# Layer 1's blocks 2 to 5 as two more pairs, and the second batch's transform beside the first pairs

## The chip, the cores and the metric

The kernel runs on one core of a Trainium2 chip. The metric is the device time in microseconds of one execution. Times are medians of several runs; the profile is of one execution, taken by the hardware profiler.

## The reference

The inputs are x (2 batches of 3008 tokens, 256 channels), a filter in the frequency domain, and two layers of weights, each 256 to 2048 to 256. What is computed:

```
X = rfft(x, axis=1);  y = irfft(X * (filt_r + 1j * filt_i), n=3008, axis=1)
h = y @ w_in1;  g = where(h >= 1, h, where(h <= -1, 0, (h + 1)**2 / 4));  z = g @ w_out1
h = z @ w_in2;  out = (h * sigmoid(h)) @ w_out2
```

All is in fp32. Both batches together are 6016 tokens.

## The kernel before, in words

**Precision.** TensorE has a slow fp32 form and a fast one that rounds (fp32r). Most products use the fast one: each operand is split into a rounded part and its remainder, and three matmuls are summed (`triple`): high by high, high by low, low by high. Splitting takes one ScalarE copy (rounding) and one subtraction on VectorE or GpSimd.

**The transform.** The 3008 tokens of a batch are 47 x 64. An item is 16 channels of one batch, 32 items in all. It goes through three products: `fwd_n1`, a VectorE transpose (`turn_fwd`), `fwd_n2`, the filter (`filter_`, two products on VectorE with the filter and with its signed half, `signs` on GpSimd), a swap of halves on ScalarE with an addition on GpSimd (`swap_add`), `inv_n2`, and a transpose into the store Z (`turn_inv`). The last product of the inverse, `last_stage`, is made for each block of tokens just before the block is used. `HEAD` items (17) run at the start, in fp32, one after another. The other 15 run in the split form beside layer 1; their stages stand in `BSTAGES`, as offsets from a start that moves on by `SP` / 10 slots an item. There they use the rotating ring of four PSUM banks `h` and, for the padded inverse, the bank `b1` (`clear_pads`).

**Layer 1.** The tokens are 12 blocks of about 500, two to a pair (`PAIRS`). The hidden 2048 columns are 16 weight blocks (`NFC`). Blocks 0 to 5 (`NS` = 6) run directly, in 96 slots: a slot is one block of tokens and one weight block, with six matmuls up (`up`), the activation (ramp and square on ScalarE, minimum and maximum on VectorE), a split, and six matmuls down (`down`) five slots later. Each block is made ready by `prep_x`.

**Pairs.** Blocks 6 to 11 run as pairs. A step (`step`, `Group`) takes one pair of blocks and two weight blocks, and computes the four up products by seven (Strassen's scheme in Winograd's form), 21 matmuls in place of 24; its down part stays direct in layer 1, 24 matmuls, those of the step before, put between the products (`gap`). The operands of a pair are sums of blocks (`sum_x`), split into a ring of stores (`split_x2`, `rest_x2`); the sums of weights are made beforehand (`sum_first`, `round_first`, `rest_first`). A step has three kinds of PSUM banks of the ring `h`: b, d and c. Bank b holds the running sum: the first product (`start`) goes into b, ScalarE copies it into d, product A12 is added in d; in b follow S2, a copy out (`snap`), S1, a second copy out, and S4. Bank c takes S3 and A22. Bank b alternates between two banks from step to step, so that the next step can start while the last product is still read. The fourth bank is thus the other b, which is also lent to `last_stage`.

**Layer 2** runs all six pairs, with seven products up and seven down, 42 matmuls a step, 48 steps. Its weights come as 64-bit numbers: they are fetched, turned into fp32 (`read_weight`, `form_weight`), put into DRAM (`put_weight`), and later fetched in pairs, summed, split and stored again (`stage2`, `sums2`, `round2`, `rest2`, `store2`).

**Order.** TensorE's instructions run in the order of the program. For the other engines a planner (`Planner`) holds the order: every instruction has a cost and a due time worked out back from its users, and the planner gives each engine, until a mark, the instruction that can start earliest, or one with an earlier due time that can start soon after. The agenda (`at`, `due`) sets the slot, or the quarter of a step, at which a piece of work enters the program. `NB` is the first slot's number, `GA` that of the first step of pairs (four numbers a step), `END` that of the transform's end.

Of the kernel before, what the change touches and what calls it, by code (L numbers as in the profile page):

```python
# [9 lines left out]
F32 = mybir.dt.float32  # L10
# [25 lines left out]
PAIRS = (502, 502, 500, 502, 502, 500)  # L36
# [55 lines left out]

class Op:
    __slots__ = ("engine", "fn", "need", "users", "busy", "until", "port", "due", "done", "at", "left")

    def __init__(self, engine, fn, busy, until, port):
        self.engine, self.fn, self.busy, self.until, self.port = engine, fn, busy, until, port
        self.need, self.users, self.due, self.done, self.at = [], [], 0.0, None, None


class Planner:
# [3 lines left out]
    def __init__(self, nc):  # L105
# [4 lines left out]
        self.pipe = 0.0  # L110
        self.given = 0
# [22 lines left out]
    def places(cls, ap):  # L134
# [5 lines left out]
        if end - at > 2048:  # L140
            cols, u = [(at % 512) // 32], (0, 16)
        else:
# [24 lines left out]
    def put(self, engine, method, call, args, kwargs):  # L167
# [22 lines left out]
        op.left = sum(o.done is None for o in op.need)  # L190
        op.at = len(self.ops)
# [99 lines left out]
def tile_fft_conv_moe_moe(  # L291
# [13 lines left out]
    HEAD, LAG, EARLY = 17, 5, 12  # L305
    PRODUCT = (0, 15, 16)
    SP, NBX, SZ = 27, 8, 7
# [32 lines left out]
    make_ring("xb", 2, mp, [128, 2, PMAX], F32R)  # L340
# [18 lines left out]
    x2d = dram.tile([2, 128, NTOK], F32, name="x2d")  # L359

    w2d = [dram.tile([128, 512], F32, name=f"w2d{f}") for f in range(NFC)]
# [12 lines left out]
    def fetch_weight(m, f):  # L374
        w_in, w_out = ((w_in1, w_out1), (w_in2, w_out2))[m]
        raw = rot("early" if m == 1 and f < EARLY else "raw")
# [35 lines left out]
    def split_weight(m, f, pool):  # L412
# [5 lines left out]
        (nc.vector if f in (1,) else nc.gpsimd).tensor_tensor(wl, a, wh.bitcast(F32), ALU.subtract)  # L418
# [5 lines left out]
    def clear_pads(tag):  # L424
        zps.clear()
        for j in range(2 if tag == "a" else 1):
# [55 lines left out]
    def fwd_n1(i):  # L482
        st[i] = rot("h")
# [11 lines left out]
    def fwd_n2(i):  # L495
        ps = rot("h")[:, :XS]
# [15 lines left out]
    def swap_add(i):  # L512
# [7 lines left out]
        nc.gpsimd.tensor_tensor(yf, yf, s, ALU.add)  # L520
        st[i] = y

    def inv_n2(i):
        z = zps[i % len(zps)][:, :, :K1]
# [7 lines left out]
    def turn_inv(i):  # L532
# [3 lines left out]
            zps[i % len(zps)].rearrange("p d (u w) -> p d u w", w=2),  # L536
# [3 lines left out]
    NS = 6  # L540
# [46 lines left out]
    def crowded(t):  # L587

        n = 0
        for j in range(t, t + NEAR):  # L590
            n += sum(fn in (fwd_n1, fwd_n2) for fn, _ in agenda.get(j, ()))
            n += sum(fn is load_block for fn, _ in agenda.get(j, ())) * 2
            c, f = slots[j - NB] if j < GA else (0, 0)
            n += 2 * (f == (15 if c == 0 else 8) and c not in (1, NS - 1))
        return n > ROOM + (1 if B1 <= t < END else 0)

# [26 lines left out]
    def evict(o, to, ring="ob"):  # L623
# [787 lines left out]
```

## Time and profile before

| | |
|---|---|
| runs | 1078.92, 1078.98, 1079.11 us; median 1078.98 |
| profiled execution | span 1077.9 us from the first to the last instruction; its whole time isn't given apart |
| granted TensorE clock | 1.000 |
| TensorE matmuls | 4795, busy 1071.2 us |
| VectorE / ScalarE / GpSimd | busy 917.6 / 895.5 / 230.2 us |
| DMA | 131.95 MB, mean 122 GB/s |

Busy times are unions of an engine's instructions. Matmuls are pipelined and their ends are modelled, so that TensorE can look busy where it does not go at its full pace; how far one start lies behind the other tells more. All instructions of the kernel are issued through one helper and have one line, L172; they are told apart by the names of their tiles: h, o_a and o_b are PSUM banks, gh and gl the two parts of an activation, wh, wl, sh and sl those of weights and their sums, xr and xb those of operands, hl those of the transform, and names such as g, u, c, we, rawb and sl_g are free slots that hold products of a step. PE is TensorE, ACT ScalarE, DVE VectorE, POOL GpSimd, SP the engine that issues most transfers.

### The profile page before, as it was taken

How to read it: one execution, taken by the hardware profiler on the slowest of the kernel's cores; microseconds unless marked ns; L12 is line 12 of the kernel's file. 1: busy time of each engine (PE TensorE's matmuls, PEld its weight loads, DVE VectorE, ACT ScalarE, POOL GpSimd, SP SyncE). 2: the span in 40 equal slices, each digit the busy share in tenths (PEclk: the TensorE clock that was granted, in tenths of full speed). 3: DMA queues.
4: the chain of work that ended last, by engine and by line, in shares of the span. 5: the costliest groups of instructions: out<-in, count | busy, mean ns of one | idle time of the engine just before them, and what ended most of it. 6: DMA issues, size and time to landing. Idle time of an engine off the chain costs nothing.

```text
span 1077.9 us, 14639 instructions
## 1 busy us (share of the span) xinstructions
PE 1071.2 (99%) x4795; PEld 880.1 (82%) x4795; DVE 917.6 (85%) x1528; ACT 895.5 (83%) x1685; POOL 230.2 (21%) x208
## 2 busy tenths in 40 slices
PE   9999999999999999999999999999999999999998
PEld 4688888888888888888888888888888888888886
DVE  7989667677779686768888789999999999999998
ACT  3599778888778778879998889889889888889885
POOL 5655335666522110004433000000000000000000
PEclk9999999999999999999999999999999999999999
DMA  9433133434221000115776843433334323332301
GB/s 348 161 114 118 54 131 103 151 108 152 88 88 60 20 1 1 39 40 176 237 264 221 302 165 107 146 124 100 136 122 141 131 98 122 132 113 103 130 12 38
DMA packets 60076, 131.95 MB, mean 122 GB/s; under 512 B 6112, under 2 KB 30304, under 8 KB 60000
## 3 DMA queue, kind: packets, MB, share of 16 engines
q1 hardware_dynamic: 59568, 130.75, 35.8%
q8 instruction: 37, 0.61, 0.2%
q14 instruction: 39, 0.32, 0.1%
q10 hardware_dynamic: 432, 0.27, 0.1%
HBM read 99.81 MB, written 31.20 MB: 122 GB/s over the span
## 4 chain that ended last, share of the span: by engine, by line
PE 97%; DMA 1%; ACT 1%; DVE 0%; issue 0%; SPq 0%; DVEq 0%
PE h L172 48%; PE o_a L172 27%; PE o_b L172 23%; DMA Z<-in_x_dram 1%; ACT gh L172 0%; DVE c L172 0%; ACT c L172 0%; ACT rawb L172 0%; DVE xr L172 0%; DVE ob L172 0%; ACT g L172 0%; SPq L172 0%; DVE sl_raw L172 0%; DVEq L1402 0%; DVE gl L172 0%
## 5 line engine op out<-in xcount | busy, mean ns | idle before, releaser
L172 PE MATMUL h<-xr,ur 128*128 128x502 f32 (+1 forms) x816 | 226.9, 389 | 0.0
L172 PEld LDWEIGHTS h<-xr,ur 128*128 128x128 f32 x816 | 153.6, 189 | 32.1 <-ACT sl_g L172 0.4
L172 PE MATMUL o_a<-gh,wh 128*128 128x502 f32 (+1 forms) x390 | 152.2, 390 | 0.0
L172 PE MATMUL o_a<-gh,wl 128*128 128x502 f32 (+1 forms) x390 | 152.2, 390 | 0.0
L172 PE MATMUL o_a<-gl,wh 128*128 128x502 f32 (+1 forms) x390 | 152.1, 390 | 0.0
L172 PE MATMUL o_b<-gh,wh 128*128 128x502 f32 (+1 forms) x284 | 110.9, 390 | 0.0
L172 PE MATMUL o_b<-gh,wl 128*128 128x502 f32 (+1 forms) x284 | 110.7, 390 | 0.0
L172 PE MATMUL o_b<-gl,wh 128*128 128x502 f32 (+1 forms) x284 | 110.6, 389 | 0.0
L172 DVE TENSOR_TENSOR gl<-h,gh 128x502 fp32r<-128x502 f32 (+1 forms) x122 | 82.3, 675 | 24.4 <-ACT gh L172 22.4
L172 DVE TENSOR_TENSOR gl<-sl_g,gh 128x502 fp32r<-128x502 f32 (+1 forms) x137 | 91.1, 675 | 5.9 <-ACT gh L172 5.7
L172 ACT ACTIVATE gh<-sl_g 128x502 fp32r<-128x502 f32 (+1 forms) x137 | 84.0, 618 | 11.1 <-PE o_a L172 5.0
L172 ACT ACTIVATE u<-h 128x502 f32<-128x502 f32 (+1 forms) x122 | 71.5, 587 | 21.9 <-PE h L172 20.6
L172 PEld LDWEIGHTS o_a<-gl,wh 128*128 128x128 f32 x390 | 73.5, 188 | 15.4 <-DVE gl L172 0.3
L172 PEld LDWEIGHTS o_a<-gh,wl 128*128 128x128 f32 x390 | 73.4, 188 | 15.1
L172 PEld LDWEIGHTS o_a<-gh,wh 128*128 128x128 f32 x390 | 73.5, 188 | 14.9
L172 DVE SCALAR_TENSOR_TENSOR h<-u,h 128x502 f32<-128x502 f32 (+1 forms) x84 | 56.6, 680 | 27.4 <-ACT u L172 27.0
L172 ACT ACTIVATE gh<-h 128x502 fp32r<-128x502 f32 (+1 forms) x122 | 71.4, 585 | 7.4 <-DVE h L172 4.4
L172 ACT ACTIVATE u<-u 128x502 f32<-128x502 f32 (+1 forms) x115 | 71.4, 623 | 2.3 <-DVE u L172 0.3
L172 POOL TENSOR_TENSOR w2s<-w2s 128x448 fp32r<-128x448 f32 x32 | 41.8, 1325 | 139.7 <-DVE w2s L172 103.2
L172 PE MATMUL h<-xb,wh 128*128 128x502 f32 (+1 forms) x212 | 65.7, 391 | 0.1
L172 PEld LDWEIGHTS o_b<-gh,wl 128*128 128x128 f32 x284 | 53.4, 188 | 11.1
L172 PEld LDWEIGHTS o_b<-gh,wh 128*128 128x128 f32 x284 | 53.5, 188 | 10.7
(416 smaller groups left out, 2606.8 us busy)
## 6 DMA issues: line engine op xcount, KB each, us to landing
ur<-w2u SPq DMA_DIRECT2D x48, 896.0 KB, 4.8
f<-in_filt_dram SPq DMA_DIRECT2D x32, 384.0 KB, 4.6
w2u<-w2s SPq DMA_DIRECT2D x16, 448.0 KB, 2.8
Z<-in_x_dram SPq DMA_DIRECT2D x16, 256.0 KB, 5.8
xin<-in_x_dram SPq DMA_DIRECT2D x16, 256.0 KB, 3.8
raw<-in_moe_w_in_dram SPq DMA_DIRECT2D x16, 256.0 KB, 2.8
raw<-in_moe_w_out_dram SPq DMA_DIRECT2D x16, 256.0 KB, 3.0
w2d<-wa SPq DMA_DIRECT2D x16, 256.0 KB, 3.5
```

The lines of the kernel that those rows point to most:

```text
L172: op = Op(engine, lambda: call(*args, **kwargs), busy, until, port)
```

## The change

Only blocks 0 and 1 stay direct (`NS` = 2, 32 slots). Blocks 2 to 5 become two pairs that run ahead of the other three, so that layer 1 has five pairs, 40 steps. Their tokens belong to the first batch: `stage_block` computes their `last_stage` during the first 16 slots and keeps blocks 2 and 3 in the free store of the second batch, and blocks 4 and 5 in DRAM (`x1d`). The sums of weights no longer have a store each: they are written to DRAM (`w1s`) and loaded for each step from the ninth on into one of three buffers (`load_sum`).

The second batch's transform starts with the pairs, not beside the direct slots. It has 16 items (`HEAD` = 16), one in three quarters of a step, and one PSUM bank (`bank`, `begin_side`) for all three products. For the first 15 steps (`SOLO`) the step therefore has only three banks: the start goes into d, and ScalarE copies it into b (`follow`) once the activation of the step before has read b; the activation of b is written into a slot, and a group of down products (`gap(4)`) moves from before S4 to behind it. The transform's filter has one buffer in place of two. Six free slots hold a step's products at first, in place of eleven. Layer 2's weights are fetched and formed from 62 quarter steps after the first step on (`L2C`), and combined after that. The planner gives the sums and splits of the first pairs an earlier due time (`wish`). The core of the diff:

```diff
-PAIRS = (502, 502, 500, 502, 502, 500)
+PAIRS = (502, 500, 502, 502, 500, 502)
...
+        now = self.clock["PE"]
+        for op in self.ops[self.given:]:
+            if op.engine == "PE":
+                now = max(now, op.due)
+            elif op.wish is None:
+                op.wish = now + WISH
         for op in reversed(self.ops[self.given:]):
             if op.done is None:
                 due = min((u.due for u in op.users if u.done is None), default=1e9) - op.until
                 if op.engine != "PE":
-                    op.due = min(due, t + 15.0)
+                    op.due = min(due, op.wish, t + 15.0)
...
-    HEAD, LAG, EARLY = 17, 5, 12
-    PRODUCT = (0, 15, 16)
-    SP, NBX, SZ = 27, 8, 7
+    HEAD, LAG = 16, 5
+    PRODUCT = (0, HEAD - 2, HEAD - 1)
...
-        (nc.vector if f in (1,) else nc.gpsimd).tensor_tensor(wl, a, wh.bitcast(F32), ALU.subtract)
+        (nc.vector if f in (0, 1) else nc.gpsimd).tensor_tensor(wl, a, wh.bitcast(F32), ALU.subtract)
...
+    def bank():
+        return side[0] if side else rot("h")
...
-        st[i] = rot("h")
+        st[i] = bank()
...
-        z = zps[i % len(zps)][:, :, :K1]
+        zb[i] = zps[i % 2] if i < HEAD else bank().rearrange("p (d k) -> p d k", k=32)
+        z = zb[i][:, :, :K1]
...
-    NS = 6
+    NS = 2
...
-    PL = [(0, p) for p in range(NS // 2, len(PAIRS))] + [(1, p) for p in range(len(PAIRS))]
+    PL = [(0, p) for p in range(1, len(PAIRS))] + [(1, p) for p in range(len(PAIRS))]
...
+    def stage_block(n, k):
+        t = BLOCKS[n][1]
+        ps = last_stage(n, k)
+        if n < 4:
+            to = Z[1][:, k * 1024 + (n - 2) * t:k * 1024 + (n - 1) * t]
+        else:
+            to = rot("ob")[:, :t]
+        if k == 0:
+            nc.scalar.activation(to, ps, AF.Copy)
+        else:
+            nc.vector.tensor_copy(to, ps)
+        if n >= 4:
+            nc.sync.dma_start(x1d[k, :, (n - 4) * t:(n - 3) * t], to)
...
+        sh, sl = (sums_[j % 3][:, i] for i in range(2))
+        nc.sync.dma_start(w1s[j], sums_[j % 3].bitcast(F32))
+
+    def load_sum(q):
+        nc.sync.dma_start(sums_[q % 3].bitcast(F32), w1s[q % NP])
...
     def first_slots():
-        for i in range(4):
-            c = late.tile([128, PMAX], F32, name=f"c{i}")
-            retired.append(c.name)
-            spare(c)
         for tag in "gu":
             for i in range(2):
                 spare(rings[tag][(turn.get(tag, 0) + 1 + i) % 2])
         spare(rings["we"][0].bitcast(F32))
+        spare(wa3)
...
-            self.b, self.d, self.c = h[q % 2], h[2], h[3]
-            self.other = rings["h"][1 - q % 2]
+            self.solo = q < SOLO
+            self.b, self.d, self.c = h[0 if self.solo else q % 2], h[2], h[3]
+            self.other = rings["h"][1 if self.solo else 1 - q % 2]
...
         def start(self):
+            if self.solo:
+                self.prod(self.d, "A11", "B11", True)
+                return
+            if self.q == SOLO:
+                mark_written(rings["h"][2])
             self.prod(self.b, "A11", "B11", True)
             nc.scalar.activation(self.d, self.b, AF.Copy)
+
+        def follow(self):
+            if self.solo:
+                nc.scalar.activation(self.b, self.d, AF.Copy)
...
-                if self.m or not IN_BANK or (name == "b" and any(fn is load_block for fn, _ in agenda.get(GA + 4 * self.q + 4, ()))):
+                if self.m or (name == "b" and (self.solo or any(fn is load_block for fn, _ in agenda.get(GA + 4 * self.q + 4, ())))):
...
-        gap(4)
+        if not k.solo:
+            gap(4)
         k.prod(k.b, "S4", "B22", False)
         k.act("b", k.b)
         if k.m:
             k.combine()
+        if k.solo:
+            gap(4)
         gap(5)
+        if q + 1 < STEPS:
+            groups[q + 1].follow()
...
+    GA = NB + W1S
+    Y = GA + 4 * NP * L2P
+    B1, SP = GA, 30
     BSTAGES = (
-        (-5, (load_x,)), (-2, (load_f,)), (0, (fwd_n1, turn_fwd)), (3, (fwd_n2, filter_)),
-        (7, (inv_n2, turn_inv)), (4, (swap_add,)), (1, (split_st,)), (5, (split_st,)),
-        (1, (signs,)), (-2, (split_x,)),
+        (-6, (load_x,)), (0, (fwd_n1, turn_fwd, split_st)), (7, (inv_n2, turn_inv)),
+        (2, (fwd_n2, filter_, swap_add)), (4, (split_st,)), (1, (signs,)),
+        (-1, (load_f,)), (-1, (split_x,)),
     )
     for i in range(HEAD, n):
         t = B1 + SP * (i - HEAD) // 10
         for d, fns in BSTAGES:
             for fn in fns:
                 at(t + d, fn, i)
-    at(B1 - 3, split_mats)
-    END = B1 + SP * (n - 1 - HEAD) // 10 + SZ + 2
+    at(B1 - 5, split_mats)
+    END = B1 + SP * (n - 1 - HEAD) // 10 + 8
+    L2C = GA + 62
+    SOLO = (END - GA) // 4 + 1 | 1
...
+    for n_ in range(2, 6):
+        for k in range(2):
+            at(NB + 2 + 2 * (2 * (n_ - 2) + k), stage_block, n_, k)
...
-        t = NB + (34 + 4 * f if f < EARLY else 85 + 2 * (f - EARLY))
+        t = L2C + 3 * f
...
-        t = GA + 44 + 9 * j // 2
+        t = L2C + 12 + 11 * j if j < 3 else GA + 110 + 6 * (j - 3)
...
+    nine = {"B11": 12, "B21": 14, "T2": 26, "T3": 28, "T1": 29, "B22": 29, "T4": 30}
+    held = END - GA - 4 * NP
+    after = {"B11": held + 4, "B21": held + 5, "T2": 27, "T3": 28, "T1": 29, "B22": 29, "T4": 30}
+    sums_after = {"T1": held + 6, "T2": held + 6, "T3": held + 7, "T4": held + 7}
...
-            open_dp("dpb", 2, 2, 1, 1)
-            make_ring("early", 1, dp, [128, 512], I64)
+            open_dp("dpb", 2, 1, 1, 1)
+            rings["s"].append(rings["ob"][0][:, :XS])
+            rings["obs"] = rings["ob"][1:]
...
+    def begin_side():
+        side.append(rings["h"][1])
...
+    for q in range(NP, NP * L2P):
+        at(GA + 4 * (q - 3) + 3, load_sum, q)
```

## Rows read from the trace of the kernel before

**Rows 1.** The page, part 1: busy us (share of the span) x instructions.

```profile
PE 1071.2 (99%) x4795; PEld 880.1 (82%) x4795; DVE 917.6 (85%) x1528; ACT 895.5 (83%) x1685; POOL 230.2 (21%) x208
```

**Rows 2.** The page, part 4: shares of the chain that ended last, by engine.

```profile
PE 97%; DMA 1%; ACT 1%; DVE 0%; issue 0%; SPq 0%; DVEq 0%
```

**Rows 3.** Stretches: us, then busy (x) of PE PEld DVE ACT POOL, clock, DMA, GB/s.

```profile
20.00:40.00 20.00, 20.00 (x57) 10.64 (x56) 20.00 (x29) 10.72 (x21) 18.27 (x20) 1.00 0.92 316
50.17:138.00 87.83, 87.82 (x400) 72.59 (x400) 70.71 (x112) 77.12 (x146) 40.31 (x34) 1.00 0.29 93
160.00:300.00 140.00, 140.00 (x670) 119.65 (x669) 102.52 (x173) 115.51 (x214) 85.39 (x77) 1.00 0.36 116
440.00:480.00 40.00, 40.00 (x200) 34.13 (x199) 25.10 (x43) 29.57 (x56) 0.00 (x0) 1.00 0.16 53
500.00:560.00 60.00, 60.00 (x265) 49.70 (x264) 50.72 (x86) 58.37 (x117) 22.64 (x18) 1.00 0.71 234
640.00:1040.00 400.00, 400.00 (x1762) 331.72 (x1761) 387.26 (x645) 351.55 (x659) 0.00 (x0) 1.00 0.35 118
```

**Rows 4.** Timeline of PE: start, length, tile, count; first products of two steps.

```profile
398.79 0.62 PE L172 MATMUL h<-xr,wh 128*128 128x502 f32 x2
...
409.06 0.62 PE L172 MATMUL h<-xr,wh 128*128 128x502 f32 x2
```

**Rows 5.** Timeline of PE in the head: first products of two items.

```profile
17.11 1.02 PE L172 MATMUL h<-Z,fwd 128*128 128x512 f32 x2
...
19.26 1.02 PE L172 MATMUL h<-Z,fwd 128*128 128x512 f32 x2
```

**Rows 6.** Timeline of PE, transform beside slots: second product, first product, next slot.

```profile
199.32 0.51 PE L172 MATMUL o_b<-hl,fwd_hi 128*128 128x384 f32 x2
...
199.85 0.63 PE L172 MATMUL h<-hl,fwd_hi 128*128 128x512 f32 x2
...
200.54 0.62 PE L172 MATMUL h<-xb,wh 128*128 128x502 f32 x2
```

**Rows 7.** Timeline at the first slot: first weight's remainder and its first reader.

```profile
49.01 1.27 POOL L172 TENSOR_TENSOR wl<-wa,wh 128x512 fp32r<-128x512 f32 x1 [0.74 <-ACT wh L172]
...
50.71 0.39 PE L172 MATMUL h<-x,wl 128*128 128x502 f32 x1
```

**Rows 8.** DMA issues from 140 to 300 us: KB each, median us to landing.

```profile
f<-in_filt_dram SPq DMA_DIRECT2D x14, 384.0 KB, 3.2
```

**Rows 9.** Timeline, quiet step: third matmul of S1, and the second snapshot.

```profile
444.33 0.39 PE L172 MATMUL h<-xr,wl 128*128 128x502 f32 x1
...
444.76 0.59 ACT L172 ACTIVATE rawb<-h 128x502 f32<-128x502 f32 x1 [1.09 <-PE h L172]
```

**Rows 10.** Timeline, two loaded steps: third matmul of S1, snapshot; in the first S4.

```profile
491.35 0.39 PE L172 MATMUL h<-xr,wl 128*128 128x502 f32 x1
...
492.57 0.60 ACT L172 ACTIVATE rawb<-h 128x502 f32<-128x502 f32 x1
...
493.63 0.62 PE L172 MATMUL h<-xr,sh 128*128 128x502 f32 x2
...
573.62 0.38 PE L172 MATMUL h<-xb,wl 128*128 128x500 f32 x1
...
575.00 0.58 ACT L172 ACTIVATE u<-h 128x500 f32<-128x500 f32 x1
```

**Rows 11.** Groups: count | busy us, mean ns | idle before; square, minimum, copy between banks.

```profile
L172 ACT ACTIVATE u<-u 128x502 f32<-128x502 f32 x79 | 49.1, 624 | 1.5 <-DVE u L172 0.3
...
L172 DVE SCALAR_TENSOR_TENSOR h<-u,h 128x502 f32<-128x502 f32 (+1 forms) x84 | 56.6, 680 | 27.4 <-ACT u L172 27.0
...
L172 ACT ACTIVATE h<-h 128x502 f32<-128x502 f32 x48 | 27.7, 577 | 2.2 <-PE h L172 1.3 <-DVE gl L172 0.7
```

**Rows 12.** Timeline of PE: first products of a loaded step and of the next.

```profile
486.43 0.62 PE L172 MATMUL h<-xb,wh 128*128 128x502 f32 x2
...
497.05 0.62 PE L172 MATMUL h<-xb,wh 128*128 128x502 f32 x2
```

More of the change, by code (lines that the diff above doesn't have):

```diff
@@ L90, in _constants @@
     return dft.astype(np.float32)
+WISH = 6.0
 class Op:
-    __slots__ = ("engine", "fn", "need", "users", "busy", "until", "port", "due", "done", "at", "left")
+    __slots__ = ("engine", "fn", "need", "users", "busy", "until", "port", "due", "done", "at", "left", "wish")
     def __init__(self, engine, fn, busy, until, port):
@@ L141, in places @@
             cols, u = [(at % 512) // 32], (0, 16)
+        elif at // 512 != (end - 1) // 512:
+            cols, u = range(16), (at // 512, (end - 1) // 512 + 1)
         else:
@@ L339, in tile_fft_conv_moe_moe @@
     make_ring("x", 2, mp, [128, 2, PMAX], F32R)
-    make_ring("xb", 2, mp, [128, 2, PMAX], F32R)
+    rings["xb"] = [mp.tile([128, 2, PMAX], F32R, tag=f"xb{i}", name=f"xb{i}", bufs=1) for i in range(2)]
     make_ring("wa", 3, rawp, [128, 512], F32)
@@ L591, in crowded @@
             n += sum(fn in (fwd_n1, fwd_n2) for fn, _ in agenda.get(j, ()))
[L592 to L595, printed above, removed]
+            n += sum(fn in (load_block, stage_block) for fn, _ in agenda.get(j, ())) * 2
+        return n > ROOM
     def act_rest(u, h, g):
@@ L814, in split_x2 @@
         n, v = size(p), operand(p, which)
-        h, l = (r[:, :n] for r in ring[(7 * p + USE.index(which)) % len(ring)]())
+        ring.append(ring.pop(0))
+        h, l = (r[:, :n] for r in ring[-1])
         nc.scalar.activation(h, v, AF.Copy)
@@ L894, in give @@
             t = self.slot.pop(name)
-            if not (self.q >= Q2 - 1 and t.tensor.name in retired):
+            if t.tensor.name not in retired:
                 free.append(t)
@@ L1194, in tile_fft_conv_moe_moe, with keep_slot @@
         at(Y - 24 + 4 * (t // 2), load_down, t)
+    xring2 = [rings["xb"][1][:, s] for s in range(2)]
+    def keep_slot():
+        nonlocal wa3
+        wa3 = rings["wa"].pop()
+    wa3 = None
+    at(GA - 5, keep_slot)
     def make_xring():
@@ L1210, in tile_fft_conv_moe_moe @@
         at(s, load_pair, p)
-        if PL[p][0] == 0:
+        if PL[p][0] == 0 and p > 1:
             for i in range(2):
-                if p:
-                    for k in range(2):
-                        at(t + (8 if p == 1 else 4) + 4 * i + k, load_block, p, i, (k,))
-                else:
-                    at(s + i, load_block, p, i)
-        for which, d in (sums_later if p else sums).items():
+                for k in range(2):
+                    at(t + (held + 2 * i if p == 2 else 4 + 4 * i) + k, load_block, p, i, (k,))
+        for which, d in (sums_after if p == 2 else sums_later if p else sums).items():
             at(t + d, sum_x, p, which)
-        for which, d in (later if p else first).items():
+        for which, d in (after if p == 2 else nine if p in (3, 4, 5) else later if p else first).items():
             at(t + d, split_x2, p, which)
             at(t + d + 1, rest_x2, p, which)
-    dctx = ExitStack()
+    dctx, lctx, sctx = ExitStack(), ExitStack(), ExitStack()
     DP = ("xin", "f", "t1", "y", "s")
@@ L1318, in tile_fft_conv_moe_moe @@
     h_ring()
-    rings["h"] = [rings["h"][j] for j in (0, 3, 1, 2)]
-    mark_written(rings["h"][2])
+    rings["h"] = [rings["h"][j] for j in (1, 3, 0, 2)]
+    begin_side()
+    mark_written(rings["h"][0])
     groups[0] = Group(0)
     groups[0].start()
+    groups[0].follow()
     down(*slots[-LAG])
@@ L1352, in tile_fft_conv_moe_moe @@
             lctx.close()
+            sctx.close()
+            v = mp.tile([128, 2, PMAX], F32R, tag="xb1", name="xb2", bufs=1)
+            ring.insert(0, [v[:, s] for s in range(2)])
             gp = ctx.enter_context(tc.tile_pool(name="gp", bufs=1))
```

160 lines of the change are left out of this document (93 added, 67 removed).

## The prediction

> **What bounds the kernel now.** I read the engine shares first, then the chain that ended last, then busy time by stage, then single steps. TensorE is busy for 1071.2 of the 1077.9 us span [rows 1], and 97% of the chain is TensorE [rows 2]. Its matmul ends are modelled, so I checked the pace by starts. From 640 to 1040 us there are 1762 matmuls, one of them cut by the window's edge: 400 / 1761 = 0.227 us for one of some 502 columns [rows 3]. A step of layer 1's pair stage, 45 matmuls, runs from 398.79 to 409.06, 10.27 us or 0.228 each [rows 4]. So TensorE issues back to back, and a matmul taken out is worth its 0.227 us wherever no new wait takes its place. The clock is full (1.00) in all these windows [rows 3]. The other engines matter only through waits. ScalarE is busy for 29.6 of 40 us where the pair stage is alone, 115.5 of 140 where the second batch's transform runs beside direct slots, and 58.4 of 60 where layer 2's weights are combined; TensorE loses nothing in these three windows [rows 3].
>
> The sum is made against the profiled execution, whose span is 1077.9 us; its time with what lies around the span isn't listed. The median of the runs, 1078.98, is 1.1 above that span, and I keep this 1.1 unchanged.
>
> **1. Two more pairs in seven products.** In direct form, two weight blocks by two token blocks are four slots of 6 up and 6 down matmuls, 48. The step is 7 x 3 up and 24 down, 45. Two pairs have 16 steps: 16 x 3 = 48 matmuls fewer, 48 x 0.227 = 10.9 us. This is on the path, since the pace has no idle time in it. [...]
>
> **2. One item goes from the head to the split form.** In the head an item takes 2.15 us of TensorE (17.11 to 19.26) [rows 5]. In the split form the second product takes 0.53 us (199.32 to 199.85) and the first 0.69 (199.85 to 200.54) [rows 6]; the third has the second's width, so 0.53: 1.75 together. The head is full on TensorE and on VectorE (20.0 of 20 us each) [rows 3], and the item leaves both, so I count the difference, 0.4 us less. At its end the first weight's remainder starts at 49.01 and takes 1.27, ready at 50.28, and its first reader starts at 50.71 [rows 7]: 0.4 spare. Should TensorE come 2.15 earlier and the weight not, 2.15 - 0.4 = 1.7 us would be lost. But the weight's VectorE work stands in that full queue, and its last subtraction moves from the 1.27 us GpSimd instruction to VectorE. I take 0 and keep 1.7 for the range.
>
> **3. Work beside TensorE that costs nothing.** Eight staged half-blocks replace eight prepared ones: the same matmuls, earlier, with one copy in place of a copy and a subtraction. In their stretch ScalarE is busy for 77.1 of 87.8 us [rows 3], and the added matmuls lengthen the stretch. If that cover failed, one ScalarE instruction each, 8 x 0.6 = 5 us, would be the worst. Blocks 4 and 5 go through DRAM: written by the 16th slot and read back after the 34th, 18 slots of 12 x 0.227 = 2.7 us, 49 us apart. The reload of a step's sums (384 KB a step, three buffers) is issued on SP's queue after the step three earlier has used the buffer; a landing takes about 3.2 us for that size [rows 8], and two steps of 10 us lie before its use.
>
> **4. The fifteen steps that share PSUM.** Here one bank less is left to the pair stage, and each step has three more ScalarE instructions (two snapshots and the copy between banks) than the four slots it replaces, 15 in all, besides about one for operands. Sixteen items at three quarters of a step each bring 1.33 items a step, 5 ScalarE instructions each: 22.6 in 10.27 + 1.33 x 1.75 = 12.6 us. At 58.37 / 117 = 0.50 us [rows 3] that is 11.3, 90%: less than the window at 97% in which TensorE lost nothing. So ScalarE isn't a bound here by its sum; what counts is how late single instructions are. Two covers shrink.
>
> (a) The second snapshot reads bank b after product S1 and must end before product S4 writes there. Now three groups of three matmuls lie between, in the change two. In a quiet step the snapshot starts 0.43 us after the start of S1's third matmul (444.33 to 444.76) and takes 0.59 [rows 9]. The third matmul and six more last 7 x 0.227 = 1.59, so about 0.55 is spare. In a loaded step it starts 1.22 after (491.35 to 492.57), ends 1.82 after, and product S4, now 2.28 after (493.63), would stand at 1.60: 0.22 us late, 0.27 with the signal. Of the sixteen steps of before where the instruction can be told, three are like that; the first is this one and the last, 573.62 to 575.00, ends 0.4 late [rows 10]. Below, this costs 0; above, 0.43 in each of 15 steps, 6.5 us. Since the nearest load is a window without loss, I take three in sixteen at 0.3, 0.85 us.
>
> (b) With one bank b, product S4's result must be read through (ramp, square, minimum) and the next start copied in before product A12 overwrites that start. The chain from S4's third matmul is 0.43 + 0.59 + 0.62 + 0.68 + 0.58 [rows 9, 11] with some 0.15 of signals, 3.05 us. Over it lie that matmul, fifteen more and two of the transform's products, 16 x 0.227 + 2 x 0.53 = 4.7. Spare: 1.65, three ScalarE instructions. I take 0.15 for all steps together; if each of its four instructions stood behind one other, 3 x 0.50 + 0.59 = 2.1, each step would lose 0.45 and all 7 us.
>
> **5. Layer 2's weights move together.** All sixteen were formed beside the direct slots and only combined beside layer 1's pairs; now forming and combining both follow the transform, beside the fourth to sixth pair. Per weight that is two ScalarE and three VectorE instructions, so some 32 more ScalarE instructions of 0.50 us in about twenty steps of 10.27, 8% of them. Before, the twelve steps beside the combining had two that lost 0.4 us each, as 486.43 to 497.05 = 10.62 [rows 12] against 10.27 [rows 4]. Twenty at the same rate lose 1.4, so 0.6 more than now. The ends are 0.8 gained (no such step left) and 7 lost (all of them).
>
> **Sum.** -10.9 - 0.4 + 1.0 + 0.6 = -9.7, so the span is 1068.2 and the time 1069.3 us.
>
> **Rivals.**
> A. ScalarE is late in the snapshot of every shared step: 6.5 in place of 1.0, so 1069.3 + 5.5 = 1074.8. For it: the load is constant there at 90%, where the trace of before has it in turns. Against it: lateness near zero in 13 of 16 steps, also from 500 to 560.
> B. Slower: ScalarE's queue holds both covers up in one step. Place: bank b in the fifteen shared steps. A step then loses 0.43 for the snapshot and 0.45 for the copy, 0.88, all 13.2: 1078.98 - 11.3 + 13.2 + 0.6 = 1081.5. It decides from 11.3 / 15 = 0.75 us a step. [...] For B: an order fixed beforehand can't let an urgent copy pass. Against it: it needs two late waits in every step, with 1.65 us spare in one.
> C. The transform's single filter buffer. A new load may be issued only when the filter's two products have read the old one. Two reads on VectorE of at most 0.68 [rows 11], landing 3.2 from its issue [rows 8], the signs on GpSimd at most 1.27 as the larger instruction [rows 7]: 5.8 us in a period of three quarters of a step, 9.4. It decides when landing takes over 6.8 us; a microsecond lost for each of 16 items gives 1069.3 + 16 = 1085. Against it: 3.2 us as median [rows 8].
> D. The head's weight isn't earlier: 1069.3 + 1.7 = 1071.
>
> **Chances.** The forecast with D and its own small waits 0.65 (1066.9 to 1072.5), A 0.22 (1072.5 to 1077.5), B 0.08, C 0.05. Without any wait the time would be 1078.98 - 11.3 - 0.8 = 1066.9, so the range begins at 1066.5; it ends at 1076.5, most of A within. A difference of 0.2%, 2.2 us, is about what a measurement of this kernel can tell from no change. Faster by more holds the forecast and most of A, 0.84; slower by more, B and C beyond their points, 0.11; 0.05 lie between.
>
> **What would show it.** Step 1: about 48 matmuls of 500 or 502 columns fewer in the shares, and layer 2 beginning some 10 us earlier. Step 2: the first direct slot some 2 us earlier; a wait of TensorE on the first weights would show D. Step 4: steps of about 12.6 us between the 32nd slot and the end of the transform. Waits of TensorE's weight loads or matmuls on ScalarE just before S4 or A12 show A or B; waits on GpSimd or the filter's DMA show C. Step 5: steps of 10.6 rather than 10.2 while weights are formed. Wrong as a whole would be shared steps above 13.4 us, or any stretch in which TensorE's pace falls below 0.227 us a matmul for long.

## The result, and the profile after

The changed kernel takes 1093.76 us (median of four runs, 1092.82 to 1094.96) where the one before takes 1079.05 beside it: a ratio of 1.0137, interval 1.0123 to 1.0151. That is 14.7 us slower; the forecast was 9.7 us faster. The profiled execution took 1092.82 us, with a span of 1091.0. In these profiles all instructions stand under one line, L179, so tiles tell them apart.

The engine shares, answering [rows 1], and the shares of the chain that ended last, answering [rows 2]:

```profile
PE 1068.4 (98%) x4743; PEld 869.1 (80%) x4743; DVE 978.3 (90%) x1579; ACT 926.7 (85%) x1746; POOL 246.3 (23%) x210
```

```profile
PE 77%; DVE 10%; ACT 9%; issue 2%; DMA 1%; POOL 0%; SPq 0%; DVEq 0%; ACTq 0%; POOLq 0%
```

TensorE has 52 matmuls fewer and a longer span. Its share of the chain fell from 97% to 77%; VectorE has 10% that it did not have. VectorE's own busy time grew by 61 us, with only 51 instructions more.

The stretches that answer to [rows 3]: head, slots, the last slots, the steps beside the second batch's items, later steps, layer 2.

```profile
20.00:40.00 20.00, 20.00 (x66) 11.27 (x65) 20.00 (x30) 11.05 (x21) 18.27 (x19) 1.00 0.79 282
60.00:120.00 60.00, 60.00 (x306) 51.36 (x305) 50.79 (x77) 50.37 (x93) 30.03 (x21) 1.00 0.35 115
120.00:148.00 28.00, 25.79 (x112) 20.48 (x112) 27.22 (x48) 24.22 (x51) 16.86 (x16) 1.00 0.28 98
148.00:330.00 182.00, 172.05 (x748) 137.09 (x749) 155.41 (x244) 158.72 (x299) 100.94 (x88) 1.00 0.28 92
340.00:560.00 220.00, 219.17 (x1017) 182.62 (x1017) 198.85 (x320) 201.79 (x388) 60.05 (x45) 1.00 0.57 188
640.00:1040.00 400.00, 400.00 (x1761) 331.36 (x1760) 386.09 (x644) 351.08 (x657) 0.00 (x0) 1.00 0.35 123
```

TensorE idles mainly in two of them, 120 to 148 (2.2 us) and 148 to 330 (10); from 340 to 560 it is 0.8. A busy TensorE need not be at its pace (from 52.5 to 55.8 us, below, it is busy for 3.30 of 3.30 us with 10 matmuls at a clock of 0.50), so I also measured lost time by starts: from each matmul's start to the next one's, less the median of matmuls of its kind in the trace before (0.2275 us for 500 or 502 columns), summed by stretch.

```
lost TensorE time, us        before              after
head                         3.7 (0 to 50)       4.2 (0 to 48.5)
first slots                  0.6 (50 to 62)      4.4 (48.5 to 60)
other slots                  0.6 (62 to 350)     3.3 (60 to 148)
steps beside the items       -                   16.9 (148 to 330)
other steps of layer 1       1.2 (350 to 605)    2.4 (330 to 618)
layer 2                      0.2                 0.2
sum                          6.3                 31.4
```

Without lost time the changed kernel is 11.6 us shorter; 25.1 us of new lost time stand against that, 13.5 in all (the spans differ by 13.1). What TensorE waited for in the shared steps, by the view of its waits from 147 to 331 us (total, times, longest):

```profile
PE h L179 <- DVE y L179: 3.2, 3, 1.5
PE h L179 <- DVE gl L179: 2.4, 3, 1.4
PE h L179 <- DVE t L179: 1.4, 2, 1.2
PE o_a L179 <- DVE gl L179: 1.3, 1, 1.3
PE o_b L179 <- DVE gl L179: 1.0, 2, 0.8
PE h L179 <- ACT wa L179: 0.5, 1, 0.5
PE h L179 <- ACT h L179: 0.5, 1, 0.5
PE h L179 <- ACT g L179: 0.4, 1, 0.4
```

VectorE ends 9.3 us of them, ScalarE 1.4, a DMA none. One of the 1.5 us waits in the timeline, with GpSimd, VectorE and TensorE together:

```profile
213.21 1.36 POOL L179 TENSOR_TENSOR hl<-xin,hl 128x512 fp32r<-128x512 f32 x1
213.34 1.78 DVE L179 TENSOR_TENSOR xs<-xs 128x502 f32<-128x502 f32 x1
...
215.03 0.28 DVE L179 TENSOR_TENSOR ws<-wa,ws 128x128 f32<-128x128 f32 x1
215.24 1.01 DVE L179 TENSOR_TENSOR y<-h,f 128x384 f32<-128x384 f32 x2
...
216.30 0.73 PE L179 MATMUL h<-hl,fwd_hi 128*128 128x512 f32 x2 [1.49 <-DVE y L179]
```

GpSimd starts an item's subtraction at 213.21 and ends at 214.57. VectorE starts a difference of two SBUF tiles at 213.34, which alone takes 0.67, and ends it at 215.12, 0.55 after GpSimd's end. The filter's two reads of the side bank stand behind it in VectorE's queue, and the next item's first product waits for them until 216.30. It is no single case. Over the whole trace, 70 VectorE instructions of 500 or 502 columns with two SBUF inputs start while a GpSimd instruction runs: they take 1.05 us on the median, and 67 of them end 0.53 to 0.55 us after that instruction does. The 741 that meet none, and the 33 that start before GpSimd does, take 0.67; so do the 85 that read PSUM and start while GpSimd runs. That is what the trace shows; what in the chip causes it, no run shows.

The same operation in two forms, VectorE's groups by shape from 150 to 320 us (count, busy us, mean ns, idle before):

```profile
L179 DVE TENSOR_TENSOR gl<-u,gh 128x500 fp32r<-128x500 f32 x8 | 8.3, 1034 | 0.3 <-ACT gh L179 0.2
...
L179 DVE TENSOR_TENSOR gl<-h,gh 128x500 fp32r<-128x500 f32 x8 | 5.4, 672 | 2.5 <-ACT gh L179 2.2
```

Reading a bank (h) it takes 672 ns, reading SBUF twice (u, gh) 1034 beside GpSimd. The trace before showed this too, in groups that I had not read, beside the items from 160 to 300 us:

```profile
L172 DVE TENSOR_TENSOR gl<-h,gh 128x502 fp32r<-128x502 f32 x17 | 11.4, 671 | 4.4 <-ACT gh L172 4.4
...
L172 DVE TENSOR_TENSOR gl<-g,gh 128x502 fp32r<-128x502 f32 x4 | 3.7, 916 | 0.1
```

There the direct slots leave their values in PSUM; only 5 of 39 such subtractions read SBUF twice, four of them at 916 ns. The pairs keep their values in SBUF: of all VectorE instructions 15 of 172 have two SBUF inputs in that stretch of before, and 121 of 268 in the fifteen shared steps of the change. So the change put the same GpSimd work beside VectorE instructions that it held up.

### The profile page after: what moved, and what is told of

Its sections match the earlier page's. It is cut to its first block, busy times and chain, and to the rows that moved or that the text cites. A ratio compares the mean times of both kernels' runs of the same rounds, so it can differ in the third digit from the quotient of the medians.

```text
span 1091.0 us, 14799 instructions
## 1 busy us (share of the span) xinstructions
PE 1068.4 (98%) x4743; PEld 869.1 (80%) x4743; DVE 978.3 (90%) x1579; ACT 926.7 (85%) x1746; POOL 246.3 (23%) x210
## 4 chain that ended last, share of the span: by engine, by line
PE 77%; DVE 10%; ACT 9%; issue 2%; DMA 1%; POOL 0%; SPq 0%; DVEq 0%; ACTq 0%; POOLq 0%
PE h L179 39%; PE o_a L179 21%; PE o_b L179 17%; DVE gl L179 2%; ACT gh L179 2%; ACT u L179 1%; DVE wa L179 1%; ACT g L179 1%; DMA Z<-in_x_dram 1%; DVE u L179 1%; ACT wa L179 1%; DVE h L179 1%; DVE g L179 1%; ACT sl_xb L179 1%; ACT we L179 1%
## 5 line engine op out<-in xcount | busy, mean ns | idle before, releaser
L179 PE MATMUL h<-xr,ur 128*128 128x502 f32 (+1 forms) x792 | 220.8, 389 | 0.0
L179 PEld LDWEIGHTS h<-xr,ur 128*128 128x128 f32 x792 | 149.0, 189 | 31.2 <-ACT sl_g L179 0.4
L179 PE MATMUL o_a<-gl,wh 128*128 128x502 f32 (+1 forms) x358 | 139.6, 390 | 1.3 <-DVE gl L179 1.3
L179 PE MATMUL o_a<-gh,wh 128*128 128x502 f32 (+1 forms) x358 | 139.9, 391 | 0.0
L179 PE MATMUL o_a<-gh,wl 128*128 128x502 f32 (+1 forms) x358 | 139.6, 390 | 0.0
L179 PE MATMUL o_b<-gl,wh 128*128 128x502 f32 (+1 forms) x316 | 123.5, 391 | 1.1 <-DVE gl L179 1.0
L179 PE MATMUL o_b<-gh,wh 128*128 128x502 f32 (+1 forms) x316 | 123.6, 391 | 0.0
L179 PE MATMUL o_b<-gh,wl 128*128 128x502 f32 (+1 forms) x316 | 123.2, 390 | 0.0
L179 DVE TENSOR_TENSOR gl<-sl_g,gh 128x502 fp32r<-128x502 f32 (+1 forms) x137 | 90.9, 673 | 5.9 <-ACT gh L179 5.7
L179 ACT ACTIVATE gh<-sl_g 128x502 fp32r<-128x502 f32 (+1 forms) x137 | 83.9, 618 | 10.8 <-PE o_a L179 5.8
L179 PE MATMUL h<-xr,wh 128*128 128x502 f32 (+1 forms) x288 | 89.7, 393 | 1.0 <-ACT h L179 0.5
L179 PE MATMUL h<-xr,sum 128*128 128x502 f32 (+1 forms) x312 | 88.3, 391 | 0.9 <-ACT wa L179 0.5
L179 PEld LDWEIGHTS o_a<-gl,wh 128*128 128x128 f32 x358 | 67.4, 188 | 14.9 <-DVE gl L179 1.9
L179 PEld LDWEIGHTS o_a<-gh,wl 128*128 128x128 f32 x358 | 67.3, 188 | 13.7
L179 PEld LDWEIGHTS o_a<-gh,wh 128*128 128x128 f32 x358 | 67.5, 188 | 13.1
L179 PEld LDWEIGHTS o_b<-gl,wh 128*128 128x128 f32 x316 | 59.5, 188 | 14.0 <-DVE gl L179 2.7
L179 PEld LDWEIGHTS h<-xr,sum 128*128 128x128 f32 x312 | 58.5, 188 | 14.5 <-ACT wa L179 1.8
L179 PEld LDWEIGHTS o_b<-gh,wl 128*128 128x128 f32 x316 | 59.5, 188 | 12.2
L179 PEld LDWEIGHTS o_b<-gh,wh 128*128 128x128 f32 x316 | 59.5, 188 | 11.5
L179 PEld LDWEIGHTS h<-xr,wh 128*128 128x128 f32 x288 | 53.2, 188 | 14.8 <-ACT h L179 1.2
L179 ACT ACTIVATE u<-h 128x502 f32<-128x502 f32 (+1 forms) x94 | 54.8, 582 | 10.6 <-PE h L179 8.2
L179 ACT ACTIVATE u<-u 128x502 f32<-128x502 f32 (+1 forms) x100 | 61.9, 619 | 1.8 <-DVE u L179 0.6
```

What stands on the lines that cost most here:

```text
L179: op = Op(engine, lambda: call(*args, **kwargs), busy, until, port)
```

## The experiments

All edits are to the changed kernel; each time stands with its ratio to the kernel before on the same chip. The planner orders everything anew after an edit, and near variants differ by up to 2 us in the shared steps for that alone, so small differences carry nothing.

**The wait at the first slot.** After the change the first weight's remainder is VectorE's:

```profile
50.85 1.70 DVE L179 TENSOR_TENSOR wl<-wa,wh 128x512 fp32r<-128x512 f32 x2
...
51.77 0.49 PE L179 MATMUL h<-x,wl 128*128 128x502 f32 x1 [2.53 <-DVE wl L179]
```

It answers to [rows 7], where 0.4 us were spare. Behind this wait the granted clock is 0.50 (windows, columns as in [rows 3], the clock before the last two):

```profile
48.50:52.10 3.60, 1.07 (x6) 0.62 (x5) 3.45 (x7) 1.49 (x3) 1.28 (x1) 1.00 0.44 146
52.50:55.80 3.30, 3.30 (x10) 2.59 (x9) 1.94 (x5) 2.27 (x4) 0.00 (x0) 0.50 0.43 151
```

First try, the remainder back on GpSimd:

```
-        (nc.vector if f in (0, 1) else nc.gpsimd).tensor_tensor(wl, a, ...)
+        (nc.vector if f in (1,) else nc.gpsimd).tensor_tensor(wl, a, ...)
```

> The changed kernel with one thing undone: the first weight's remainder is again subtracted on GpSimd. In the changed kernel TensorE waits 2.5 us for that remainder at 51.8 us and then runs at the lower clock to 55.6 us (1.4 us more). Theory H (the subtraction stands on VectorE behind four subtractions of prepared blocks): both go, 1093.8 - 3.9 = about 1090. Rival (the weight itself is not earlier, since its steps stand at the same numbers while the head is one item shorter): under 1.5 us gained, 1092.5 or more.

1097.17 us, 1.0164 [1.0147, 1.0181]. The wait grew to 3.40: GpSimd's subtraction takes 1.45 and starts late too (50.55). Which engine does it is not the cause.

Second try, all of layer 1's weights one slot earlier (`CP` 12 to 13):

> The changed kernel with every weight of layer 1 fetched, formed and split one slot earlier (CP 13 in place of 12), so that the weights' steps stand to the end of the head as they did before, when the head had one item more. Putting the first remainder back on GpSimd alone did not help (1097.2). Theory D (the weights stood at the same numbers while the head became one item shorter, so TensorE reaches the first slot before them): the wait of 2.5 us and most of the 1.4 us at the lower clock behind it go, 1093.8 - 3.5 = about 1090. Rival (VectorE's order at that place, with four subtractions of prepared blocks ahead of the remainder, is the cause whatever the slot): the wait stays over 2 us, 1093 to 1095.

1094.37, 1.0144 [1.0126, 1.0162]; the wait is 2.54, as without the edit, and the rival holds. With fp32 items (below) the same edit:

> Both of the above: the items beside the pairs in plain fp32, and the weights of layer 1 one slot earlier. If the two losses are separate, the gains add: 1084 to 1088 under theories D and L together; still above the kernel before (1079.3).

1087.14, 1.0071 [1.0055, 1.0087]: within the range, but no gain over e_f32 (1085.67) either. VectorE's order had not moved: the weight's last forming step behind the head's last transpose, its remainder behind four remainders of x. Third try, which does move it:

```
-        late = [2, 1][f] if f < 2 else 0
+        late = [0, 1][f] if f < 2 else 0
```

> The changed kernel, with the forming of layer 1's first weight two slots earlier (its delay of 2 set to 0), so that VectorE gets its last forming step before the last two transposes of the head and its remainder before the four remainders of x. Theory O (VectorE's order at the head's end): the wait of 2.53 us at 51.77 goes, and with it the half clock behind it (about 1.5 us): 1089 to 1091 us. Rival (the wait only moves: to a late transpose in the head, or to the second weight's remainder): 1092.5 to 1095.

The wait and the low clock went from there, and the third slot starts at 53.48 in place of 55.58. The same window has twice the matmuls:

```profile
52.50:55.80 3.30, 3.30 (x20) 2.87 (x20) 2.34 (x5) 3.11 (x6) 1.30 (x1) 1.00 0.01 2
```

But the time is 1093.61, 1.0135 [1.0118, 1.0152]: nothing gained. The rival held, at a place I had not named. The first pair begins at 147.99 (147.84 in the changed kernel); the 2 us come back before it, in a new wait with the low clock behind it:

```profile
129.66 1.84 DVE L179 TENSOR_TENSOR gl<-h,gh 128x502 fp32r<-128x502 f32 x3
```

```profile
130.38 0.84 PE L179 MATMUL h<-x,wh 128*128 128x502 f32 x2 [2.68 <-DVE gl L179]
```

```profile
130.90:134.20 3.30, 3.30 (x9) 2.60 (x9) 3.30 (x6) 3.02 (x8) 3.08 (x3) 0.50 0.38 121
```

From 120 to 148 us VectorE is busy for 27.2 of 28 us in the changed kernel (above): it prepares the first pair beside the last slots, and it sets when the pair starts. GpSimd has a part in this too: the 25 VectorE instructions with two SBUF inputs there take 5.1 us more than their like that meet no GpSimd instruction. What that costs the time is not shown; no run took GpSimd's work away there. With that preparation spread (sums, copies and remainders one to three slots earlier) on top of e_late0:

> e_late0 (weight 0 formed two slots earlier), and the sums, copies and remainders of the first pair's operands one to three slots earlier each, the sums of its weights six earlier. If VectorE's backlog of 120 to 148 us set when the first pair starts, TensorE's 5.5 us of lost time there falls to 2 to 3 and the time to 1089.5 to 1091.5. Rival (the work only collides earlier, with the weights' forming at 60 to 120 us, or the shared steps take it back): 1092.5 to 1095.

1092.20, 1.0119 [1.0104, 1.0134], between the two ranges. The first pair begins at 145.16, 2.7 us earlier than in the changed kernel, and lost time from 120 to 148 is 3.9 in place of e_late0's 5.5 (3.1 in the changed kernel). Against the changed kernel 1.6 us are gained by the medians, but the runs overlap (1091.15 to 1093.08 and 1092.82 to 1094.96).

**The shared steps: what the items cost.** Three theories stood at first. P: GpSimd's work lengthens VectorE's instructions that read SBUF twice, and VectorE is late for TensorE. A: ScalarE's queue is late, as in rivals A and B. R: with single banks each step is a chain of waits, whatever the load. Later L stands for the load as such, C for the chain of product, copy, subtraction and next product through one bank, O for VectorE's order at the head's end, G and Q for GpSimd's and ScalarE's share of the split's work. The items left out altogether (the second half of the output is then not computed):

> The changed kernel with the second batch's transform left out (its 16 items beside the pairs; the later pairs read what the store holds), while the first 15 steps keep their three banks and their order. TensorE loses 16 x 1.75 = 28 us of matmuls. Theory R: the waits of the three-bank step stay, some 12 to 17 us: 1093.8 - 28 = 1062 to 1066. Theories P and A: without the items' work the three-bank step has no loss (10.2 to 10.4 us a step): 1093.8 - 28 - 17 = about 1049.

1052.62, 0.9753 [0.9734, 0.9773]: 41 us for 16 items of some 1.75 us, 28 us [rows 6]. R's 12 to 17 us do not stay, but the loss does not vanish either, as P and A have it: these steps lose some 6.5 us without items, 5.3 of it in the first seven. The largest part is one wait on ScalarE with the low clock behind it:

```profile
160.59 0.71 PE L179 MATMUL h<-xr,wh 128*128 128x500 f32 x2 [2.02 <-ACT h L179]
```

```profile
161.40:164.70 3.30, 3.30 (x9) 2.64 (x8) 0.88 (x2) 1.85 (x4) 0.71 (x1) 0.50 0.30 119
```

So one bank less explains at most a part of the 16.9, and the items the rest.

The swap's two ScalarE copies per item left out (the halves are then added unswapped):

```
-        nc.scalar.activation(s[0:64], v[64:128], AF.Copy)
-        nc.scalar.activation(s[64:128], v[0:64], AF.Copy)
...
-            nc.gpsimd.tensor_tensor(s, yf, s, ALU.add)
+            nc.gpsimd.tensor_tensor(s, yf, v, ALU.add)
```

> The changed kernel, with the two ScalarE copies that swap halves left out for each of the 16 items beside the pairs (the addition reads the unswapped product): 32 ScalarE instructions, 16 us, fewer in the shared steps; GpSimd and VectorE as before. Theory A: ScalarE's load there falls from about 90% to 81%, so most of its lateness goes: about half of the 17 us, 1085. Theory P: 1091 to 1094. Theory R: 1091 to 1094.

1096.21, 1.0156 [1.014, 1.0171], no gain with 17 us less of ScalarE's work. By itself this does not clear ScalarE, because VectorE got slower: from 150 to 320 us its 230 instructions take 154.0 us in place of 146.6, those with two SBUF inputs being held up longer (table below). What speaks against theory A is that ScalarE ends 1.4 us of TensorE's waits (above), and e_f32_copies (below).

The items' GpSimd subtractions left out (the low parts are then missing, the high part is used twice):

```
-        nc.gpsimd.tensor_tensor(parts[1], src, parts[0].bitcast(F32), ALU.subtract)
-        return parts
+        return [parts[0], parts[0]]
```

> The changed kernel, with the three remainders of each of the 16 items beside the pairs left out (the rounded part is used in their place, so TensorE's matmuls are as many); GpSimd loses 48 instructions of about 1.2 us, VectorE and ScalarE none. Theory P (GpSimd's work lengthens VectorE's instructions that read two operands from SBUF, 0.83 to 0.89 us on the mean in place of 0.68, and VectorE is then late for TensorE): that mean falls below 0.75, TensorE's lost time from 148 to 330 us falls from 17 to under 8 us, the time to 1085 or less. Theory A (ScalarE's queue is late, as in rival B of the prediction): ScalarE's work is unchanged, 1092 to 1094. Theory R (the single banks make each step a chain of waits, whatever the load): 1091 to 1094, a little from shorter item chains.

1088.88, 1.0091 [1.0076, 1.0106]: 4.9 us gained, less than P expected and more than A and R. The same subtractions on VectorE:

```
-        nc.gpsimd.tensor_tensor(parts[1], src, ...)
+        nc.vector.tensor_tensor(parts[1], src, ...)
```

> The changed kernel with the three remainders of each item beside the pairs on VectorE in place of GpSimd: 48 instructions of some 0.6 us, 29 us, more for VectorE in the shared steps, 57 us less for GpSimd. Theory P (lengthening by GpSimd's work is what makes VectorE late): about as the run without remainders, 1089 to 1092. Theory L (VectorE's load is what makes it late): its busy share in the shared steps rises from 85% to some 95%, lost time by 5 us or more, 1098 to 1110.

1095.76, 1.0152 [1.013, 1.0174]: no gain, since VectorE then has 42 instructions more in the same stretch. It leaves P and L undecided.

Items without the split, in plain fp32 products (more TensorE time, no copies, no subtractions):

```
-        (0, (fwd_n1, turn_fwd, split_st)), ... (4, (split_st,)), ... (-1, (split_x,)),
+        (0, (fwd_n1, turn_fwd)), ...
-    at(B1 - 5, split_mats)
```

> The changed kernel with the 16 items beside the pairs in plain fp32, not split: three rounding copies on ScalarE (22 us in all) and three subtractions on GpSimd (57 us) go for 48 each, VectorE's instructions stay, and TensorE's products take 2.15 in place of 1.75 us an item, 6.4 us more in all. The run without remainders lost 14.0 us in the shared steps in place of 17.0, so GpSimd alone explains 3. Theory L (VectorE and ScalarE together are loaded so that in-order instructions come late at the short covers of the single banks): lost time in the shared steps falls to 5 to 9 us, 1093.8 + 6.4 - 8 to 12 = 1088 to 1092. Theory P alone: 14 us remain, 1093.8 + 6.4 - 3 = 1097.

1085.67, 1.0062 [1.0044, 1.008]: 8.1 us faster, below L's range, though TensorE has some 16 x 0.40 = 6.4 us more to do. So about 14 us of waiting hang on the split. Is it the work itself, or that the copy and the subtraction stand between two products? The same kernel with the work put back, its results unread:

> The second batch's items run their products in fp32, as in e_f32, but each item still issues its three ScalarE copies, its three GpSimd subtractions and the split of the matrices; nothing reads what they write. So the work is there, only not between two products of an item. Theory L (the load: 16 x 3 copies of 0.5 to 0.6 us on ScalarE and 16 x 3 subtractions of 1.1 to 1.5 us on GpSimd, with the lengthening of VectorE's instructions beside them): the 13 us that e_f32 gained beyond its 6.4 us of TensorE's time come back, 1095 to 1100 us. Theory C (the chain: the copy and the subtraction stand between one product and the next, which all go through one side bank): the time stays at e_f32's, 1084 to 1088, though GpSimd is as busy as in the changed kernel. In between (1089 to 1094): both.

1096.21, 1.0157 [1.0142, 1.0172], 10.5 us of the 14 are back: mostly L. And the split kept for the 512-column product alone:

> Only the two products of 384 columns of each item run in fp32; the 512-column one keeps its split, whose copy and subtraction depend on nothing but the loaded input and are issued one gap earlier, so they stand outside the chain through the bank. TensorE saves about 16 x 0.17 = 2.7 us against e_f32. Theory C: 1082 to 1084 us, since the chain is as short as in e_f32. Theory L: a third of the copies and subtractions is back, about a third of 13 us less the 2.7 saved: 1086 to 1089.

1089.56, 1.0101 [1.0086, 1.0116]: above C's range, just past the end of L's. With e_late0 added, no sum of gains:

> e_f32_384 and e_late0 together. If C and O hold and add up: 1078 to 1081 us, level with the kernel before. If O fails: as e_f32_384. If L holds in place of C: 1082 to 1086.

1091.41, 1.0114 [1.0098, 1.0129]. Then the put-back work in two halves, ScalarE's copies alone and GpSimd's subtractions alone:

> fp32 products with the items' three ScalarE copies (and those of the matrices) issued as work that nothing reads, and no GpSimd subtraction for them. Theory G (GpSimd's subtractions are what costs, by lengthening VectorE's instructions that read two SBUF operands): near e_f32, 1085 to 1088 us. Theory Q (the copies cost: each waits in ScalarE's queue for its input, and snapshots and the copies of the remainders stand behind it): 1091 to 1096 us. Half and half: 1089 to 1091.

1087.95, 1.0084 [1.0067, 1.0101].

> The counterpart: fp32 products, the items' three GpSimd subtractions issued (each reads its item's tile twice, nothing reads the result), no ScalarE copies for them. G: 1091 to 1096 us, and VectorE's 500-column subtractions again at 0.85 to 0.9 us in place of 0.68. Q: 1085 to 1088.

1095.27 (1092.39 to 1096.23), 1.0143 [1.0128, 1.0159]. The subtractions cost 9.6 us, the copies 2.3: theory G. The windows from 150 to 320 us (columns as in [rows 3]), in the order changed kernel, e_nopool, e_f32, e_f32_copies, e_f32_subs:

```profile
150.00:320.00 170.00, 160.05 (x695) 126.98 (x694) 146.60 (x230) 147.84 (x279) 97.81 (x85) 1.00 0.29 96
```

```profile
150.00:320.00 170.00, 162.77 (x709) 129.30 (x708) 139.46 (x233) 149.57 (x283) 40.13 (x41) 1.00 0.30 96
```

```profile
150.00:320.00 170.00, 167.55 (x677) 126.94 (x677) 140.51 (x238) 134.16 (x247) 42.63 (x41) 1.00 0.31 99
```

```profile
150.00:320.00 170.00, 166.70 (x671) 125.09 (x670) 139.77 (x235) 150.93 (x289) 43.75 (x41) 1.00 0.31 99
```

```profile
150.00:320.00 170.00, 161.14 (x640) 118.72 (x639) 146.90 (x231) 128.77 (x235) 86.95 (x85) 1.00 0.30 99
```

Divide VectorE's busy time (third pair) by its count: 0.637, 0.599, 0.590, 0.595, 0.636 us. It is 0.64 where GpSimd has some 85 instructions and 0.59 to 0.60 where it has 41, whatever ScalarE does (279, 283, 247, 289, 235). The group of 1034 ns above shows it singly, in e_nopool:

```profile
L179 DVE TENSOR_TENSOR gl<-u,gh 128x500 fp32r<-128x500 f32 x8 | 5.8, 727 | 0.6 <-ACT gh L179 0.3
```

And the wait that follows from it, in e_f32_subs (GpSimd, VectorE, TensorE):

```profile
221.03 1.31 POOL L179 TENSOR_TENSOR ob<-y,ob 128x384 f32<-128x384 f32 x1
...
221.41 1.46 DVE L179 TENSOR_TENSOR gl<-we,gh 128x500 fp32r<-128x500 f32 x1
...
222.93 0.49 PE L179 MATMUL o_b<-gl,wh 128*128 128x500 f32 x1 [1.47 <-DVE gl L179]
```

VectorE ends 0.53 after GpSimd (222.34 to 222.87), and TensorE's down product starts at once.

Another reading would be that GpSimd itself is late, with the swap's additions and the filter's signs standing behind the subtractions. The waits do not bear it out: VectorE waits for GpSimd for 1.0 us in all in the changed kernel (147 to 331) and for nothing in e_f32_subs, and TensorE waits for it in neither.

The fifteen shared steps take 13.6 us on average ((97.9 + 106.2) / 15), over the 13.4 that I had named as the sign of a wrong forecast; the first step after the items takes 10.24 (351.98 to 362.22), as in [rows 4]. The loss is not spread evenly. The table has the length of steps 1 to 7 and 8 to 15, counted by their up products. The last two columns add up how much longer VectorE's instructions with two SBUF inputs (70 and 51; in e_dve 95 and 74) take than the median of the same operation and shape that does not start while GpSimd runs:

```
us                length of steps      VectorE lengthened
                  1 to 7   8 to 15     1 to 7   8 to 15
changed kernel      97.9     106.2       12.9       5.5
e_nopool            94.1     107.0        3.9       2.6
e_noswap           101.9     104.3       19.6       9.4
e_dve              101.2     106.7        7.9       2.3
e_f32_384           99.4     102.9       11.2       1.9
e_f32               93.8     103.9        4.2       2.5
e_f32_copies        96.2     104.2        6.6       1.2
e_f32_subs         102.5     103.9       15.1       4.0
e_f32_load         100.3     106.2       12.2       7.3
```

VectorE's other instructions are lengthened by 0.2 us at most in any of these stretches. In the first seven steps VectorE also forms the sums of layer 1's weights, and is busy for 90% of them in the changed kernel. There the length follows the lengthening, in the split forms and in the fp32 forms each (e_dve has 25 VectorE instructions more): the subtractions cost 8.7 us (e_f32_subs against e_f32), or 3.8 with the split in use (changed kernel against e_nopool). In steps 8 to 15, where VectorE is busy for 79%, they cost nothing in either. There the changed kernel stays 2.3 above e_f32 although its products take some 3 us less (16 x 0.40, spread evenly over the steps), so some 5 in all. The chain (C) is a part of this: e_nopool, with the copies between the products and no subtractions, takes 107.0, e_f32_copies, with the same copies unread, 104.2, and e_f32_384, whose copy and subtraction stand before the chain, 102.9. Load may be another part, since e_f32_load, without the chain, is 2.3 above e_f32 too. That rests on these comparisons alone; no run isolated it.

The best of the parts together, fp32 items with both edits of e_early:

> e_f32 with both edits of e_early. If they add up: 1080.5 to 1083 us, still above the kernel before (its 6.4 us of fp32 products and about 4 us in the shared steps remain). If the early preparation gains nothing: 1085 to 1087.

1084.34, 1.0047 [1.0032, 1.0062], between the two ranges: the fastest form of the change, still slower than the kernel before. None of the versions that compute the whole output beats it.

## Why the prediction was wrong

**Step 1** was right, and step 2's arithmetic with it: 52 matmuls fewer, 48 of them of 500 or 502 columns (4248 to 4200), and 11.6 us less at full pace against 11.3.

**Step 2, rival D.** The first slot came 1.6 us earlier (48.55) and waited, as D has it, but the price was mis-sized: 2.53 us of waiting and a clock of 0.50 behind it, 3.8 us of new lost time where I took 0 and bounded 1.7. As I read it, the 17th item's products had covered the head's last transpose and the weight's forming steps; no run gave that item back. e_late0 then showed that this price hardly counts by itself, because VectorE sets when the first pair starts.

**Step 3** failed. I weighed ScalarE in that stretch (it held: 24.2 of 28 us), not VectorE, whose preparation of the first pair now stands beside the last of far fewer slots: 2.7 us of new lost time.

**Step 4** is the step that failed most. Its two covers, priced at 1.0 us, were not far off: ScalarE ends 1.4 us of TensorE's waits (in e_noitems it ends one of 2.02). What was missing is VectorE. I added up ScalarE's load (90% forecast, 158.7 / 182 = 87% measured) and took the stage as bounded by it; I never counted VectorE's instructions, nor asked whether they keep their length beside GpSimd. Those with two SBUF inputs became 18.4 us longer in these steps (12.9 and 5.5), and VectorE ends 9.3 us of TensorE's waits. The lost time is 16.9 us, and a step takes 13.6 us where 12.6 were forecast.

**Step 5** was about right: other steps of layer 1 lost 1.2 us more, forecast 0.6.

**Rivals.** A and B name ScalarE. TensorE waits on it for 1.4 us, and putting the items' copies back costs 2.3 (e_f32_copies against e_f32), well below A's 6.5 and B's 13.2; the time lies beyond B's 1081.5 by another mechanism. C did not decide: the filter's transfers land in 3.1 us on the median and 4.2 at most, below its 6.8. GpSimd waits for them for 4.4 us in five places, and one lies in the chain that ended last, but TensorE waits for none. I had no rival for VectorE and GpSimd, and the range had no room for it.

Open: why taking GpSimd's subtractions away gains 4.9 us in the split form and putting them back costs 9.6 in the fp32 form. VectorE's lengthening in steps 1 to 7 differs less (9.0 and 10.9), so more of it reaches TensorE in the fp32 form; and 1.5 of the 9.6 arise before the first pair, which begins at 148.69 in e_f32_subs and at 147.15 in e_f32.

## What to carry to other kernels

When work is moved beside other work, list for every engine what it would do there, not only for the one that looks fullest, and see where each VectorE operand lies: here the same subtraction took 1034 ns on the mean with two SBUF inputs beside GpSimd (from 150 to 320 us) and 672 with one of them from PSUM. The trace before had the price, in a small group of four at 916 ns beside twenty-eight at 670. A wait cured at one place pays only if no other engine sets the next stage's start; look at that engine's busy share first.

## What the runs showed of the hardware

In the trace of the changed kernel 67 of the 70 VectorE instructions of 500 or 502 columns with two SBUF inputs that started while a GpSimd instruction ran ended 0.53 to 0.55 us after it (as at 213.34 above, and at 221.41 in e_f32_subs). The 70 took 1.05 us on the median and 1.80 at most, where their like that met no GpSimd instruction took 0.67; the 33 that started before GpSimd did, and the 85 that read PSUM, stayed at 0.67 to 0.68 on the median beside the same work. After TensorE's wait of 2.53 us at the first slot the granted clock was 0.50 from 52.5 to 55.8 us: 10 matmuls, where e_late0 without that wait has 20 at 1.00. It was 0.50 for 3.3 us again behind the wait of 2.68 us in e_late0 and behind that of 2.02 in e_noitems.
